# Half of the Strassen differences of a fused attention + MoE kernel taken by GpSimd instead of VectorE

## Chip, cores and metric

One core of a Trainium2 chip. The metric is the device time of one execution in microseconds, from the first to the last instruction on the core with what lies around them; lower is better.

## What is computed

Three layers follow each other. The first is a linear attention: softmax over the head's own 64 columns of q, softmax of k over the sequence, then `q (k^T v)`.

```python
q_s = exp(q - max(q)); q_s = q_s / (sum(q_s) + 1e-9)          # over the head dimension
k_s = exp(k - max(k)); k_s = k_s / (sum(k_s) + 1e-9)          # over the sequence
x   = einsum(q_s, einsum(k_s, v))      # 8 x 8 heads, 576 positions, 64 columns -> 4608 x 512
h   = x @ moe_w_in;   y = (max(h, 0) ** 2) @ moe_w_out        # 512 -> 2048 -> 512
h   = y @ moe2_w_in;  out = elu(h) @ moe2_w_out               # 512 -> 2048 -> 512
```

All of it is float32. A product in float32 is made of three fast products: each operand is split into a high part (rounded by ScalarE) and a low part (what is left, by VectorE), and hi·hi, hi·lo and lo·hi are added up in PSUM.

## The kernel before, in words

The 4608 tokens are cut into nine blocks of 512 (t = 0 to 8). Block 0 goes alone; blocks 1 and 2, 3 and 4, 5 and 6, 7 and 8 are pairs. The first layer's up-projection (`up`, lines 539 to 558) makes G = relu(h)² of a block: 16 tiles of 128 rows by 512 tokens. In a pair these are four quarters, B11 and B21 of the left block (rows 0 to 1023 and 1024 to 2047), B12 and B22 of the right one, each in four pieces of 128 × 1024 (k = 0 to 3).

The down-projection of a pair is done by Strassen-Winograd's scheme with seven products in place of eight. Its right-hand operands are B11, B21, B22 and four differences, taken by `t_sum(to, k)` (line 617), piece by piece:

- T3 = B22 − B12, into a buffer of its own
- T1 = B12 − B11, into B12's place
- T2 = B22 − T1, into B11's place (B11 has been multiplied by then)
- T4 = B21 − T2, into B21's place (B21 has been multiplied by then)

The seven products are 56 **units** (u = 0 to 55), eight of each, in the order T3, T1, B11, B22, T2, B21, T4 (`SEVEN`, line 606). One unit (`unit`, line 1156) does this: `u_mm` (line 652), six matmuls of 512 columns on TensorE (PE) with the weights that `u_load` fetched; the differences that `pair_steps` (line 706) put on this unit; then `u_split(t, u + 2)` (line 642), which makes the operands of the unit after next: `uh` on ScalarE (ACT), then `ul` = x − uh on VectorE (DVE). `uh` and `ul` have three buffers each, so `uh` of unit u can be written once unit u − 3 is through PE.

The order of the work on each engine is written out by hand: the program order is the queue of each engine. Between the units stand steps of the attention of later blocks (`extras`: q and k and v loads, `q_max`, `q_sub`, `q_norm` on DVE, transposes and small products on PE) and, in the last pair, the first steps of the second layer (`x2_sum`, `x2_split`). GpSimd (POOL) has memsets (`v_load`, line 245, and `kv_mm`, line 279) and the issue of some DMAs. `v_load` is issued in two halves: two memsets on POOL, then the load on the queue of SP.

The numbers that the change touches stand in `pair_steps`: the units on which each piece of T1, T2 and T4 is put. T2's piece k is read by `u_split` of units 32 + 2k and 33 + 2k, T4's by that of units 48 + 2k and 49 + 2k. A piece of T2 overwrites what `u_split` of units 16 + 2k and 17 + 2k read, a piece of T4 what that of 40 + 2k and 41 + 2k read.

Of the kernel before, what the change touches and what calls it, by code (L numbers as in the profile page):

```python
# [13 lines left out]
ALU = mybir.AluOpType  # L14
# [6 lines left out]
def tile_attention_moe_moe2(  # L21
# [18 lines left out]
    nc = tc.nc  # L40
# [42 lines left out]
    def xf_slot(i, name):  # L83

        return keep.tile([P, 2 * TB], F32, tag=f"xf{i}", name=name)
# [336 lines left out]
    def attention(t):  # L422

        slots, put = plan()
        new = [b for b, _, _ in pieces(t) if b not in begun]
        begun.update(new)

        far = t > 1
        for b in new:
            for p in range(NP):  # L430
                for i, f in (
                    (0, kt_load), (2, k_max), (5, k_load), (5, v_load), (8, k_row), (8, k_sub), (9 + far, k_exp),
                    (11 + far, kv_mm), (11 + far, kv_sum), (11 + far, kv_inv), (11 + 2 * far, kv_out),
                ):
                    put(i + 4 * p, f, b, p)
        for s in range(NS):
            put(s // 2, q_load, t, s)
            for i, f in (
                (2, q_max), (3, q_sub), (4 + far, q_exp), (5 + 2 * far, q_sum), (6 + 2 * far, q_eps),
                (7 + 2 * far, q_inv), (7 + 2 * far, q_norm),  # L440
            ):
                put(i + 5 * s, f, t, s)
        turns = ((26, 28), (27, 29), (28, 30), (29, 31)) if far else ((23, 25), (25, 27), (27, 29), (28, 29))
        for p, (i, j) in enumerate(turns):
            put(j, x_mm, t, p)
            put(i, x_tr, t, p)
        return slots
# [169 lines left out]
    def t_sum(to, k):  # L617
        if to == "T3":
            x = xf_slot(k % 2, f"T3_{k}").rearrange("p (i n) -> p i n", n=TB)
            a, b = bq["B22", k], bq["B12", k]  # L620
        elif to == "T1":
            x = a = bq["B12", k]
            b = bq["B11", k]
        elif to == "T2":
            x, a, b = bq["B11", k], bq["B22", k], bq["T1", k]
        else:
            x = a = bq["B21", k]
            b = bq["T2", k]
        nc.vector.tensor_tensor(x, a, b, op=ALU.subtract)
        bq[to, k] = x  # L630

    UNITS = {4: "T3", 3: "T1", 0: "B11", 6: "B22", 2: "T2", 1: "B21", 5: "T4"}
# [73 lines left out]
    def pair_steps(t, last):  # L706

        steps = {}

        def put(u, f, *a):  # L710
            steps.setdefault(u, []).append((f, a))

        for to, us in (("T3", (None, None, None, 2)), ("T1", (3, 5, 7, 9)), ("T2", (17, 19, 21, 23)), ("T4", (44, 46, 48, 50))):
            for k, u in enumerate(us):
                if u is not None:
                    put(u, t_sum, to, k)
        put(9, u_keep, t, 4, 0, None)
        put(20, u_v, t)
        put(25, u_keep, t, 0, 0, 1)
        put(33, u_keep, t, 6, 1, 2)  # L720
        if not last:
            put(40, u_keep, t, 2, 0, 3)
        for m in range(2):
            if last:
                put(40 + m, u_out, t, 6, 0, 0, t + 1, m)
                put(42 + m, u_out, t, "v", 0, 1, t + 1, m)
                put(51 + m, u_out, t, 0, 1, 0, t, m)
        if last:
            put(27, u_move, t)
        else:  # L730
            for p, u in enumerate((51, 53, 55, 55)):
                put(u, x_split, 0, t + 2, p)
        return steps
# [333 lines left out]
    with tc.manual_schedule():  # L1067
# [21 lines left out]
        x = attention(PAIRED + 1)  # L1089
        place_all(x[:2], [(0, "c", NSL - 2)])  # L1090
        place_all(x[2:], firsts[PAIRED][:-2])
        for t in range(PAIRED, NB - 2, 2):
            seconds = [(t, "s", s) for s in range(NU // 2)]
            x = attention(t + 2)
# [3 lines left out]
            x = attention(t + 3)  # L1098
# [71 lines left out]
        for t in range(NB):  # L1170
            paired, final = t >= PAIRED, t == NB - 1
            right = paired and (t - PAIRED) % 2 == 1
            for j in range(NFC):
# [4 lines left out]
                if paired:  # L1178
                    if pend:
                        down(*pend.pop(0))  # L1180
                    if right and j in (10, 12):
                        t_sum("T3", (j - 10) // 2)
                    if right and j > 12:

                        u_split(t - 1, j - 13)
                    if right and j == NFC - 1:
                        for u in range(4, 12):
                            u_load(t - 1, u)
                        t_sum("T3", 2)
                    run(extras.get((t, "u", j), ()))  # L1190
                    if right and j == NFC - 3:

                        u_load(t - 1, 2)
                        u_load(t - 1, 3)
                    continue
# [14 lines left out]
            if right:  # L1210
                steps = pair_steps(t - 1, final)
                for u in range(NU - 2 if final else NU):
                    unit(t - 1, u)
# [48 lines left out]
```

## Time and profile before

| | before |
|---|---|
| runs | 1619.37, 1619.68, 1620.75 us |
| median | 1619.68 us |
| profiled execution: span from its first to its last instruction | 1615.5 us |
| what lies around the span, by the median | 4.2 us |
| PE busy | 98% of the span |
| DVE, ACT, POOL busy | 65%, 60%, 6% |
| PE clock granted | full (2.4 GHz) throughout |

The profiled execution gives only its span; its own time is taken as that span and 4.2 us. The four pairs' units lie at about 235 to 320, 421 to 505, 608 to 692 and 784 to 866 us. The second layer follows to the end.

How to read it: a row of the timeline has an instruction's start, its length, its engine, line and operation, what it writes and reads, and in brackets the idle time of the engine before it and what ended that. PEld is the weight load that precedes each matmul; it waits for the operand that the matmul will stream.

### The profile page before, as it was taken

Reading aid. Unit: us, or ns where it says so; the run is one execution under the profiler, and the core shown is the slowest. Engines: PE = TensorE matmul, PEld = TensorE weight load, DVE = VectorE, ACT = ScalarE, POOL = GpSimd, SP = SyncE. Lnnn points to the kernel's source line nnn. Section 1 sums busy time; section 2 is a strip of 40 time slices with the busy share of each in tenths; the row PEclk is TensorE's granted clock in tenths of the full one; section 3 lists DMA queues with packets and bytes.
Section 4 is the critical chain, followed back from the end, with each engine's and each line's share of the span. In section 5 each row is a group of like instructions: output and inputs, shape, how many; then the busy total and the mean of one; then the engine's idle time right before and its main releaser. Section 6 shows DMA issues by size and latency. Waiting matters only on the chain.

```text
span 1615.5 us, 22809 instructions
## 1 busy us (share of the span) xinstructions
PE 1586.3 (98%) x7958; PEld 1350.8 (84%) x7958; DVE 1051.3 (65%) x1658; ACT 974.7 (60%) x1665; POOL 90.6 (6%) x222
## 2 busy tenths in 40 slices
PE   6999999999999999999999999999999999999999
PEld 4778778878788787887888998998989999898997
DVE  7987596777877686773677554555545555555544
ACT  7996655566555675556556655555555565555544
POOL 0001220012101220011000000000000000000000
PEclk9999999999999999999999999999999999999999
DMA  7747566667775685653587555435534543543531
GB/s 264 258 156 246 197 216 198 204 210 237 257 226 174 219 289 164 201 196 111 181 288 259 197 194 173 150 110 154 171 106 143 172 129 117 190 125 109 172 112 59
DMA packets 163953, 296.17 MB, mean 183 GB/s; under 512 B 16384, under 2 KB 52224, under 8 KB 163840
## 3 DMA queue, kind: packets, MB, share of 16 engines
q1 hardware_dynamic: 154240, 263.25, 51.4%
q0 software_dynamic: 9600, 31.46, 4.9%
q8 instruction: 64, 1.05, 0.3%
q14 instruction: 49, 0.40, 0.1%
HBM read 238.03 MB, written 56.62 MB: 182 GB/s over the span
## 4 chain that ended last, share of the span: by engine, by line
PE 82%; DVE 8%; issue 5%; ACT 2%; DMA 2%; POOL 1%; SPq 1%; POOLq 0%; DVEq 0%; ACTq 0%
PE p L816 22%; PE p L661 18%; PE y L878 8%; PE y L879 8%; PE y L877 8%; PE ph L544 5%; PE ph L546 5%; PE ph L545 5%; PE px L400 2%; DVE ks L272 1%; PE pt L379 1%; PE pk L286 1%; DVE mt_wi L111 1%; DVE mt_wi L116 1%; POOL w1s L199 1%
## 5 line engine op out<-in xcount | busy, mean ns | idle before, releaser
L816 PE MATMUL p<-x2h,w 128*128 128x384 f32 x1344 | 359.6, 337 | 0.0
L661 PE MATMUL p<-uh,w 128*128 128x512 f32 x896 | 282.5, 392 | 2.9 <-DMA w<-w1s 2.9
L816 PEld LDWEIGHTS p<-x2h,w 128*128 128x128 f32 x1344 | 245.0, 188 | 4.4 <-ACT h L916 0.2
L544 PE MATMUL ph<-xh,wi0h 128*128 128x512 f32 x576 | 230.7, 401 | 0.1
L879 PE MATMUL y<-wo,g2l 128*128 128x512 f32 x576 | 226.0, 392 | 0.0
L878 PE MATMUL y<-wo,g2h 128*128 128x512 f32 x576 | 225.7, 392 | 0.0
L816 PE MATMUL p<-x2l,w 128*128 128x384 f32 x672 | 225.6, 336 | 0.0
L546 PE MATMUL ph<-xh,wi0l 128*128 128x512 f32 x576 | 225.0, 391 | 0.2 <-DVE wi0l L143 0.2
L545 PE MATMUL ph<-xl,wi0h 128*128 128x512 f32 x576 | 224.4, 390 | 0.0
L877 PE MATMUL y<-wo,g2h 128*128 128x512 f32 x576 | 224.0, 389 | 0.0
L661 PEld LDWEIGHTS p<-uh,w 128*128 128x128 f32 x896 | 168.2, 188 | 38.5 <-ACT uh L648 1.9
L918 DVE TENSOR_TENSOR h<-p,p 128x384 f32<-128x384 f32 x144 | 79.6, 553 | 183.1 <-PE p L816 181.9
L648 ACT ACTIVATE uh<-B 128x512 fp32r<-128x512 f32 x192 | 121.2, 632 | 109.4 <-PE p L661 63.7
L908 ACT ACTIVATE p<-p 128x384 f32<-128x384 f32 x144 | 69.9, 486 | 187.2 <-PE p L816 187.2
L649 DVE TENSOR_TENSOR ul<-B,uh 128x512 fp32r<-128x512 f32 x192 | 131.2, 690 | 69.3 <-ACT uh L648 68.3
L661 PE MATMUL p<-ul,w 128*128 128x512 f32 x448 | 175.3, 391 | 0.2
L553 ACT ACTIVATE B<-ph 128x512 f32<-128x512 f32 x128 | 76.2, 595 | 117.0 <-PE ph L546 116.4
L816 PEld LDWEIGHTS p<-x2l,w 128*128 128x128 f32 x672 | 126.2, 188 | 3.9
L544 PEld LDWEIGHTS ph<-xh,wi0h 128*128 128x128 f32 x576 | 109.2, 189 | 23.1 <-issue 0.9
L546 PEld LDWEIGHTS ph<-xh,wi0l 128*128 128x128 f32 x576 | 108.1, 188 | 24.1 <-DVE wi0l L143 1.1
L545 PEld LDWEIGHTS ph<-xl,wi0h 128*128 128x128 f32 x576 | 108.3, 188 | 22.8 <-issue 0.7
L879 PEld LDWEIGHTS y<-wo,g2l 128*128 128x128 f32 x576 | 108.1, 188 | 22.8
(127 smaller groups left out, 2372.1 us busy)
## 6 DMA issues: line engine op xcount, KB each, us to landing
w<-w2s SPq DMA_DIRECT2D x336, 256.0 KB, 3.0
w<-w1s SPq DMA_DIRECT2D x224, 256.0 KB, 3.4
raw_wi<-wi_dram SPq DMA_DIRECT2D x32, 512.0 KB, 4.2
raw_wo<-wo_dram SPq DMA_DIRECT2D x32, 512.0 KB, 4.0
ks<-k_dram SPq DMA_DIRECT2D x32, 320.0 KB, 4.7
vr<-v_dram SPq DMA_DIRECT2D x32, 320.0 KB, 5.6
kt<-kt_dram SPq DMA_DIRECT2D x32, 288.0 KB, 3.8
q<-q_dram SPq DMA_DIRECT2D x36, 256.0 KB, 4.7
```

The costliest lines, as they stand in the source:

```text
L544: nc.tensor.matmul(ph, hi[:, c], xh[p], start=(p == 0), stop=False)
L545: nc.tensor.matmul(ph, hi[:, c], xl[p], start=False, stop=False)
L546: nc.tensor.matmul(ph, lo[:, c], xh[p], start=False, stop=(p == NP - 1))
L553: nc.scalar.activation(g, ph, AF.Relu)
L648: nc.scalar.activation(hi, x, AF.Copy)
L649: nc.vector.tensor_tensor(lo, x, f32(hi), op=ALU.subtract)
L661: nc.tensor.matmul(accs[side, m], w[:, s, m], x, start=(new and (j, s) == (0, 0) and x is hi), stop=(j == NG - 1 and s == 1), skip_group_c ...
L816: nc.tensor.matmul(acc, w[:, s, k], x[:, k], start=(begin and (k, s) == (0, 0) and x is hi), stop=((k, s) == (1, 1)), skip_group_check=not ...
L877: nc.tensor.matmul(y2[c], gh[:, cs], hi, start=first, stop=False)
L878: nc.tensor.matmul(y2[c], gh[:, cs], lo, start=False, stop=False)
L879: nc.tensor.matmul(y2[c], gl[:, cs], hi, start=False, stop=last)
L918: nc.vector.tensor_tensor(h, part[add], part["bank", i], op=ALU.add)
```

## The change

T2 and T4 (eight pieces in each pair, 32 in all) are subtracted by GpSimd. T1 and T3 stay on VectorE. T4's pieces are put on units 40, 42, 44 and 46 in place of 44, 46, 48 and 50.

```diff
-        nc.vector.tensor_tensor(x, a, b, op=ALU.subtract)
+        eng = nc.gpsimd if to in ("T2", "T4") else nc.vector
+        eng.tensor_tensor(x, a, b, op=ALU.subtract)
         bq[to, k] = x
...
-        for to, us in (("T3", (None, None, None, 2)), ("T1", (3, 5, 7, 9)), ("T2", (17, 19, 21, 23)), ("T4", (44, 46, 48, 50))):
+        for to, us in (("T3", (None, None, None, 2)), ("T1", (3, 5, 7, 9)), ("T2", (17, 19, 21, 23)), ("T4", (40, 42, 44, 46))):
```

The queues of PE, ACT and SP keep their order. DVE, the first pair, units 40 to 52 before (`B_1_` are B21's pieces, `ul_41` the low part for unit 41, `q` and `qz` attention):

```order
L649 TENSOR_TENSOR ul_41_3226<-B_1_0_1818,uh_41_3225 128x512
L362 RECIPROCAL qz_0_3169<-qz_0_3169 128x8
L366 TENSOR_TENSOR q_0_2995<-q_0_2995,qz_0_3169 128x512
L649 TENSOR_TENSOR ul_42_3248<-B_1_1_1891,uh_42_3247 128x512
L649 TENSOR_TENSOR ul_43_3263<-B_1_1_1891,uh_43_3262 128x512
L649 TENSOR_TENSOR ul_44_3275<-B_1_2_1968,uh_44_3274 128x512
L649 TENSOR_TENSOR ul_45_3287<-B_1_2_1968,uh_45_3286 128x512
L629 TENSOR_TENSOR B_1_0_1818<-B_1_0_1818,B_1_0_1486 128x1024
L649 TENSOR_TENSOR ul_46_3300<-B_1_3_2044,uh_46_3299 128x512
L649 TENSOR_TENSOR ul_47_3312<-B_1_3_2044,uh_47_3311 128x512
L629 TENSOR_TENSOR B_1_1_1891<-B_1_1_1891,B_1_1_1582 128x1024
L649 TENSOR_TENSOR ul_48_3325<-B_1_0_1818,uh_48_3324 128x512
```

The same place on DVE in the changed kernel:

```order
L650 TENSOR_TENSOR ul_41_3226<-B_1_0_1818,uh_41_3225 128x512
L362 RECIPROCAL qz_0_3169<-qz_0_3169 128x8
L366 TENSOR_TENSOR q_0_2995<-q_0_2995,qz_0_3169 128x512
L650 TENSOR_TENSOR ul_42_3249<-B_1_1_1891,uh_42_3248 128x512
L650 TENSOR_TENSOR ul_43_3264<-B_1_1_1891,uh_43_3263 128x512
L650 TENSOR_TENSOR ul_44_3277<-B_1_2_1968,uh_44_3276 128x512
L650 TENSOR_TENSOR ul_45_3289<-B_1_2_1968,uh_45_3288 128x512
L650 TENSOR_TENSOR ul_46_3302<-B_1_3_2044,uh_46_3301 128x512
L650 TENSOR_TENSOR ul_47_3314<-B_1_3_2044,uh_47_3313 128x512
L650 TENSOR_TENSOR ul_48_3327<-B_1_0_1818,uh_48_3326 128x512
```

The 1024-column subtractions are gone from between the low parts. They stand on POOL, here in the first pair (`B_1_0_1486` and its like are T2 in B11's place, `B_1_0_1818` and its like T4 in B21's; `vr` and `kvs` are attention tiles):

```order
 L295 MEMSET kvs_3_2784 128x128
+L630 TENSOR_TENSOR B_1_0_1486<-B_2_0_2362,B_2_0_2112 128x1024
+L630 TENSOR_TENSOR B_1_1_1582<-B_2_1_2438,B_2_1_2163 128x1024
+L630 TENSOR_TENSOR B_1_2_1649<-B_2_2_2500,B_2_2_2218 128x1024
+L630 TENSOR_TENSOR B_1_3_1736<-B_2_3_2582,B_2_3_2283 128x1024
 L249 MEMSET vr_0_3111 128x5
 L250 MEMSET vr_0_3111 128x5
 L249 MEMSET vr_1_3231 128x5
 L250 MEMSET vr_1_3231 128x5
+L630 TENSOR_TENSOR B_1_0_1818<-B_1_0_1818,B_1_0_1486 128x1024
+L630 TENSOR_TENSOR B_1_1_1891<-B_1_1_1891,B_1_1_1582 128x1024
+L630 TENSOR_TENSOR B_1_2_1968<-B_1_2_1968,B_1_2_1649 128x1024
```

Eight subtractions have come into POOL's queue, four of them ahead of memsets for the next v loads, with no DMA issue between them.

## Rows read from the trace of the kernel before

**Rows 1.** The page: busy time by engine, and the chain that ended last, by engine.

```profile
PE 1586.3 (98%) x7958; PEld 1350.8 (84%) x7958; DVE 1051.3 (65%) x1658; ACT 974.7 (60%) x1665; POOL 90.6 (6%) x222
...
PE 82%; DVE 8%; issue 5%; ACT 2%; DMA 2%; POOL 1%; SPq 1%; POOLq 0%; DVEq 0%; ACTq 0%
```

**Rows 2.** Waits of PE's weight loads, 230 to 866 us: total, times, longest.

```profile
PEld p L661 <- DVE ul L649: 3.7, 12, 0.5
```

**Rows 3.** Waits of PE's weight loads in the fourth pair, 806 to 866 us.

```profile
PEld p L661 <- DVE ul L649: 1.0, 3, 0.5
```

**Rows 4.** Timeline of PEld: first weight load for the low part of units 42 and 44.

```profile
673.09 0.19 PEld L661 LDWEIGHTS p<-ul,w 128*128 128x128 f32 x1
...
675.81 0.19 PEld L661 LDWEIGHTS p<-ul,w 128*128 128x128 f32 x1
```

**Rows 5.** Timeline of DVE, third pair: low parts of units 41 to 45 (L649).

```profile
669.87 0.69 DVE L649 TENSOR_TENSOR ul<-B,uh 128x512 fp32r<-128x512 f32 x1 [0.67 <-ACT uh L648]
670.48 0.20 DVE L362 RECIPROCAL qz<-qz 128x8 f32<-128x8 f32 x1
670.71 0.69 DVE L366 TENSOR_TENSOR q<-q,qz 128x512 f32<-128x512 f32 x1
671.32 0.68 DVE L649 TENSOR_TENSOR ul<-B,uh 128x512 fp32r<-128x512 f32 x1
672.73 0.69 DVE L649 TENSOR_TENSOR ul<-B,uh 128x512 fp32r<-128x512 f32 x1 [0.72 <-ACT uh L648]
673.95 0.69 DVE L649 TENSOR_TENSOR ul<-B,uh 128x512 fp32r<-128x512 f32 x1 [0.54 <-ACT uh L648]
675.31 0.69 DVE L649 TENSOR_TENSOR ul<-B,uh 128x512 fp32r<-128x512 f32 x1 [0.67 <-ACT uh L648]
```

**Rows 6.** Timeline of ACT: high parts of units 44, 45 and 47.

```profile
673.29 0.63 ACT L648 ACTIVATE uh<-B 128x512 fp32r<-128x512 f32 x1 [0.59 <-PE p L661]
674.65 0.63 ACT L648 ACTIVATE uh<-B 128x512 fp32r<-128x512 f32 x1 [0.73 <-DVE ul L649]
...
677.37 0.63 ACT L648 ACTIVATE uh<-B 128x512 fp32r<-128x512 f32 x1 [0.73 <-PE p L661]
```

**Rows 7.** Groups of DVE by line and shape: count, busy us, mean ns, idle before.

```profile
L649 DVE TENSOR_TENSOR ul<-B,uh 128x512 fp32r<-128x512 f32 x192 | 131.2, 690 | 69.3 <-ACT uh L648 68.3
...
L629 DVE TENSOR_TENSOR B<-B,B 128x1024 f32<-128x1024 f32 x48 | 58.5, 1219 | 0.0
...
L353 DVE TENSOR_REDUCE qz<-q 128x8 f32<-128x512 f32 x34 | 23.0, 676 | 0.0
```

**Rows 8.** Groups of POOL by line and shape, the same columns.

```profile
L295 POOL MEMSET kvs<- 128x128 f32 x32 | 6.7, 217 | 9.5 <-PE px L400 9.5
L249 POOL MEMSET vr<- 128x5 f32 x32 | 3.7, 118 | 175.7 <-PE pk L286 127.1 <-issue 48.6
...
masks.py:199 POOL TENSOR_SCALAR_AFFINE_SELECT ident<-ident 128x128 f32<-128x128 f32 x1 | 0.3, 288 | 0.1
```

**Rows 9.** Timeline of DVE, first pair: T2's third piece, low parts of units 23, 24.

```profile
272.94 1.22 DVE L629 TENSOR_TENSOR B<-B,B 128x1024 f32<-128x1024 f32 x1
274.08 1.29 DVE L649 TENSOR_TENSOR ul<-B,uh 128x512 fp32r<-128x512 f32 x2
```

**Rows 10.** Timeline of all engines, first pair: weight load for the low part of unit 24.

```profile
276.08 0.19 PEld L661 LDWEIGHTS p<-ul,w 128*128 128x128 f32 x1
```

**Rows 11.** Timeline of DVE, fourth pair: low parts of units 17 and 18.

```profile
807.22 0.69 DVE L649 TENSOR_TENSOR ul<-B,uh 128x512 fp32r<-128x512 f32 x1 [0.67 <-ACT uh L648]
808.58 0.69 DVE L649 TENSOR_TENSOR ul<-B,uh 128x512 fp32r<-128x512 f32 x1 [0.67 <-ACT uh L648]
```

**Rows 12.** Timeline of POOL, first pair: memset for the v load that follows.

```profile
234.29 0.13 POOL L249 MEMSET vr<- 128x5 f32 x1
```

**Rows 13.** Timeline of SP, first pair: that v load is issued.

```profile
288.07 0.56 SPq L251 DMA_DIRECT2D vr<-v_dram x1
```

## The prediction

> **What bounds the kernel.** I read the page first: PE is busy for 98% of the span and makes 82% of the chain that ended last; DVE has 8% of that chain although it is busy for 65% [rows 1]. So work taken off DVE is worth only what PE waits for it. The view of waits says how much that is: over all four pairs the weight loads of the units waited for a low part 12 times, 3.7 us together [rows 2], and the largest share of it, 1.0 us, lies in the fourth pair [rows 3].
>
> Then the timelines, for the spare time. In the third pair a weight load for a low part comes at 673.09 for unit 42 and 675.81 for unit 44 [rows 4]: a unit takes PE 1.36 us. The low part of unit 44 starts at 673.95, ends at 674.64 [rows 5], and is wanted at 675.81 [rows 4]: 1.17 us to spare. That is the margin of nearly every low part; DVE works one unit ahead and cannot get further, since the high part in front of it waits for PE to free a buffer (673.29, released by PE) [rows 6]. A low part that comes over 1.17 us late stops PE.
>
> I take anything over 0.2% (3.2 us) as measurable for this kernel.
>
> **What the change removes.** 32 subtractions of 1.22 us leave DVE (39 us of its busy time) [rows 7]. They delay the next low part by under the margin in most places, so PE gains only the waits that they caused. I put that at 1.0 us, the fourth pair's sum [rows 3], of at most 3.7 us [rows 2]; the other waits lie mostly at T1 and at attention steps, which stay.
>
> **What it adds: the price on GpSimd.** No row shows a subtraction there, so it is bounded. A memset of 128 columns takes 217 ns and one of 5 columns 118 ns [rows 8]: 99 ns for 123 columns, 0.80 ns per column for one stream. The one operation that reads and writes, 128 columns, takes 288 ns [rows 8]: 170 ns over the small memset, 1.33 ns per column. From below it cannot be better than DVE's 1.22 us [rows 7] by anything seen here. Two reads with the write hidden are 0.12 + 1024 × 1.6 ns = 1.74 us; three streams one after the other are 0.12 + 1024 × 2.4 ns = 2.56 us; twice the read-and-write rate is 2.85 us. I take the middle of the two stream counts, **2.15 us**, which is also near 0.12 + 1024 × (1.33 + 0.80) ns = 2.30 us.
>
> **What it adds: the company of DVE.** The other unknown is what DVE's low parts do while GpSimd subtracts. From below: nothing, they keep their 0.69 us. From above: one of the two waits until the other is through. A fact of the rows speaks for the upper end: DVE takes two SBUF operands of 512 columns in 690 ns and reduces a single one in 676 ns [rows 7], so it reads two streams at once, and any path that GpSimd's two reads share with the second of them is taken. GpSimd's instructions beside the low parts so far are memsets, which read nothing [rows 8], so no row refutes it. I take the upper end. The Trainium skill says the same of this very pairing ("SBUF — State Buffer", section "Who interferes with whom"): a VectorE instruction with two SBUF inputs contends with a GpSimd instruction that reads SBUF, and the one that issues second is blocked until the first is done; no row of this trace shows it.
>
> The place matters, because GpSimd's start is tied to DVE's. A piece of T4 overwrites what the low part of unit 41 + 2k read, so it starts when that ends, just when DVE turns to the next one. Replayed on the third pair, with 2.15 us:
>
> - The low part of unit 41 ends at 670.56 [rows 5]. GpSimd holds from 670.60 to 672.75. `q_norm` (670.71) and the low part of unit 42 (671.32) [rows 5] are both two-input operations; they run after it, and the latter ends at 674.05 in place of 672.00. Its weight load is due at 673.09 [rows 4]: PE loses 1.0 us.
> - The low parts of 43 and 44 (high part ready at 673.92 [rows 6], as its buffer was freed by unit 41) follow without a gap, to 675.27. The second piece runs then, to 677.42. The high part of 45 has moved by the 1.0 us that PE lost, from 674.65 [rows 6] to 675.65; its low part ends at 678.11 and is due at 675.81 + 1.36 + 1.0 = 678.17: no loss.
> - The low part of 46 follows, the third piece goes from 678.72 to 680.87, the low part of 47 (high part 677.37 [rows 6] plus 1.0) ends at 681.56, due at 675.81 + 3 × 1.36 + 1.0 = 680.89: 0.7 us lost.
> - The fourth piece likewise, before the low part of 49: 0.7 us lost.
>
> That is 2.4 us for four pieces of T4. The other pairs have the same order of work there (in the fourth an `x2_split` stands in the place of `q_norm`): 4 × 2.4 = 9.6 us.
>
> T2: in the first three pairs PE does attention's transposes and products between these units, so the first three pieces have room. The fourth has not: with T2's third piece off DVE, the low part of unit 23 runs at 272.94 in place of 274.08 [rows 9], GpSimd goes from 273.65 to 275.80, the low part of unit 24 ends at 276.5, wanted at 276.08 [rows 10]: 0.4 us, three times 1.2 us. In the fourth pair there is no such room: the low part of unit 17 ends at 807.91, that of 18 is due to start at 808.58 [rows 11] and ends at 810.8 in place of 809.27, 1.5 us late for a margin of 1.17: 0.3 us, and then 0.7 us for two of the three that follow, as above: 1.7 us.
>
> **What is queued behind.** GpSimd's queue is in order. The memset of the next v tile, at 234.29 [rows 12], now stands behind four pieces of T2, whose last ends at about 276. Its load is issued by SP at 288.07 [rows 13], so 12 us are left. No DMA issue stands among the pieces. In the replay T4's fourth piece ends at 684.3, as unit 49 begins; it is read for unit 54, whose operands are made during unit 52. Four units later it would not have fitted.
>
> **The sum.** 9.6 + 1.2 + 1.7 − 1.0 = **+11.5 us**. On the profiled execution: 1615.5 + 11.5 = 1627.0 us of span; with the 4.2 us around it, which make up the median of the runs, 1631.2 us. With 1.74 us in place of 2.15 the first loss is 0.6 us and the later ones nearly vanish: about +3 us, 1623. With 2.56 us a piece and the two low parts behind it (1.3 us) take 3.9 us where two units have 2.72: 1.1 us lost per piece, 4.4 for a batch, five batches 22 us, 1.3 us more from T2, less 1.0: +22 us, 1642. At N = 2048 the Trainium skill gives 4497 ns for such an addition ("GPSIMD Engine Reference", section "Performance versus the Vector engine"); an estimate of half of it, 2.25 us, would put the sum at about +14 us.
>
> **The rivals.**
>
> *A. They share without loss (not slower).* DVE's low parts keep their rate beside GpSimd, or lose less than the 1.17 us that each has to spare; GpSimd takes the longer time itself, and with six units (8.2 us) between a T4 piece and its reader nobody waits. Then only the removed waits are seen: 1619.7 − 1.0, 1619 us, no change. For it: the margin, and that each piece has half a stage of time. Against it: DVE's two streams at full rate. It decides if the added delay of one low part stays under 1.17 us.
>
> *B. GpSimd is far slower.* At 2.85 us and more, T4's last piece comes after unit 52 and PE waits for it as well: 1.5 us per piece, 20 pieces, and some 2 us per pair for the last: 1655 us or more.
>
> *C. DVE was the real limit (faster).* If all 3.7 us [rows 2] and knock-on waits went, 1616 us. Against it: only part of those waits stand at T2 and T4.
>
> **How the numbers follow.** Forecast 0.48 (1623 to 1642); A 0.44; B 0.05; C 0.03. The forecast and A stand nearly level, since no row shows the two engines reading together; the forecast is ahead by DVE's two streams. Slower by over 0.2%: 0.48 + 0.05 = 0.53; within: 0.44; faster: 0.03. The range reaches from A's time, 1618.5 us, to 1642 us and leaves out B and C. The forecast's own range is 1623 to 1642.
>
> **What would show it.** Right: 32 subtractions on POOL at L630, their starts 3.6 to 4 us apart at T4; DVE's low parts beside them either starting only at GpSimd's end or stretched to over 2 us; and PE's weight loads waiting for `ul` at units 42, 47 and 49 of each pair, 10 to 15 us more in all. A is right if the low parts keep 0.69 us and those waits stay under 4 us. B shows as waits for `uh` on POOL at units 52 to 55. The forecast is wrong if GpSimd's subtraction takes under 1.6 us or if low parts run inside it.

## The result

The changed kernel took 1635.61 us (median of 4 runs, 1635.04 to 1636.42), the kernel before 1619.53 us beside it: a ratio of 1.0098, 95% interval 1.0086 to 1.0111. That is 16.1 us slower (13.9 to 18.0). The forecast was 1631 us with a range of 1618.5 to 1642.

The page of the changed kernel, answering to [rows 1]: span, busy time by engine, and the chain that ended last.

```profile
span 1634.1 us, 22844 instructions
...
PE 1594.5 (98%) x7958; PEld 1351.5 (83%) x7958; DVE 1054.6 (65%) x1626; ACT 974.5 (60%) x1665; POOL 173.2 (11%) x254
...
PE 77%; DVE 11%; issue 5%; ACT 3%; DMA 2%; POOL 1%; SPq 0%; POOLq 0%; ACTq 0%; DVEq 0%
```

DVE has 32 instructions fewer and is yet busy 3 us longer; its share of the chain rose from 8% to 11%. The groups by line and shape say why, POOL first and then DVE (columns as in [rows 7]):

```profile
L630 POOL TENSOR_TENSOR B<-B,B 128x1024 f32<-128x1024 f32 x32 | 83.1, 2597 | 231.4 <-DVE ul L650 162.8 <-DVE qz L362 67.9 <-POOL B L630 0.7
...
L650 DVE TENSOR_TENSOR ul<-B,uh 128x512 fp32r<-128x512 f32 x192 | 168.5, 896 | 80.3 <-ACT uh L649 79.2
```

A low part takes 896 ns in the mean where it took 690 [rows 7]: 37 us more in sum, which eats up nearly all of the 39 us that the 32 subtractions had taken on DVE. The low parts that stand clear of GpSimd are still 0.69 us long; the others are up to 2.9 us. Here is the place of the replay, the first piece of T4 in the third pair (timeline of DVE, answering to [rows 5], then of POOL, then of PE's weight loads, answering to [rows 4]):

```profile
680.04 0.69 DVE L650 TENSOR_TENSOR ul<-B,uh 128x512 fp32r<-128x512 f32 x1 [0.67 <-ACT uh L649]
680.65 0.20 DVE L362 RECIPROCAL qz<-qz 128x8 f32<-128x8 f32 x1
680.88 0.69 DVE L366 TENSOR_TENSOR q<-q,qz 128x512 f32<-128x512 f32 x1
681.48 2.90 DVE L650 TENSOR_TENSOR ul<-B,uh 128x512 fp32r<-128x512 f32 x1
```

```profile
680.87 2.96 POOL L630 TENSOR_TENSOR B<-B,B 128x1024 f32<-128x1024 f32 x1 [22.61 <-DVE qz L362]
685.12 2.73 POOL L630 TENSOR_TENSOR B<-B,B 128x1024 f32<-128x1024 f32 x1 [1.29 <-DVE ul L650]
688.54 2.72 POOL L630 TENSOR_TENSOR B<-B,B 128x1024 f32<-128x1024 f32 x1 [0.69 <-DVE ul L650]
691.96 2.72 POOL L630 TENSOR_TENSOR B<-B,B 128x1024 f32<-128x1024 f32 x1 [0.70 <-DVE ul L650]
```

```profile
684.43 0.19 PEld L662 LDWEIGHTS p<-ul,w 128*128 128x128 f32 x1 [1.22 <-DVE ul L650]
...
691.87 0.19 PEld L662 LDWEIGHTS p<-ul,w 128*128 128x128 f32 x1 [0.75 <-DVE ul L650]
...
695.28 0.19 PEld L662 LDWEIGHTS p<-ul,w 128*128 128x128 f32 x1 [0.78 <-DVE ul L650]
```

`q_norm` came first, the other way round than in the replay, and ended at 681.57. GpSimd's row begins at 680.87 but lasts 2.96 us, 0.57 us more than the 2.39 us of a piece that meets nobody: it waited. The low part of unit 42 was next in DVE's queue and its row of 2.90 us ends at 684.38, 0.55 us after GpSimd's end at 683.83: it waited through the whole subtraction and then did its work. A row's length here includes the wait, on both engines. The three weight loads that PE had to wait for are those of units 42, 47 and 49, the three that the replay named.

Over the four pairs (waits of PE's weight loads, 230 to 886 us, answering to [rows 2], then the whole fourth pair, 797.9 to 883.3 us):

```profile
PEld p L662 <- DVE ul L650: 19.7, 25, 1.7
```

```profile
PEld p L662 <- DVE ul L650: 7.8, 8, 1.7
```

3.7 us have become 19.7: 16.0 us more, close to the difference between the medians. Of the 7.8 us, 0.9 lie at the pair's first units, as they do before; from about unit 16 on, where [rows 3] begins, 1.0 us has become 6.9. Counted by the length of the units' own matmuls, from the first one's start to the last one's in each unit, the four pairs are 2.9, 3.2, 2.8 and 5.6 us longer, 14.5 in all.

The two spans differ by 18.6 us, 4 more than the units. Most of that has nothing to do with the change. Up to the first unit, where the two programs are alike, the profiled execution of the changed kernel is 3.5 us longer than that of the kernel before: PE's granted clock stood at 1.2 GHz for 6.8 us in block 0. A profile of the same queues with the full clock there (T4 on its old units, below) is 0.3 us longer up to that point. The stretch, after:

```profile
101.10:107.90 6.80, 5.68 (x14) 4.54 (x15) 6.29 (x13) 4.91 (x11) 0.00 (x0) 0.50 0.52 178
```

(The columns are the stretch, its length, busy us and instructions of PE, PEld, DVE, ACT and POOL, the granted clock, DMA share and GB/s.) PE did 14 matmuls there, and 29 in the same stretch of the kernel before, whose clock was full. What lies around a span is 1.7 us in this execution (1635.84 us for a span of 1634.1), not the 4.2 us taken for the kernel before; if it is as much there, the execution that was profiled before was some 2.5 us faster than the median. The forecast was added to the median and is not touched by this.

### The profile page after: what moved, and what is told of

It is laid out like the page before. It is cut to its first block, busy times and chain, and to the rows that moved or that the text cites. A ratio compares the mean times of both kernels' runs of the same rounds, so it can differ in the third digit from the quotient of the medians.

```text
span 1634.1 us, 22844 instructions
## 1 busy us (share of the span) xinstructions
PE 1594.5 (98%) x7958; PEld 1351.5 (83%) x7958; DVE 1054.6 (65%) x1626; ACT 974.5 (60%) x1665; POOL 173.2 (11%) x254
## 4 chain that ended last, share of the span: by engine, by line
PE 77%; DVE 11%; issue 5%; ACT 3%; DMA 2%; POOL 1%; SPq 0%; POOLq 0%; ACTq 0%; DVEq 0%
PE p L817 22%; PE p L662 13%; PE y L879 8%; PE y L880 8%; PE y L878 8%; PE ph L544 5%; PE ph L546 5%; PE ph L545 5%; DVE ul L650 4%; PE px L400 2%; PE pt L379 1%; DVE ks L272 1%; ACT uh L649 1%; PE pk L286 1%; DVE mt_wi L111 1%
## 5 line engine op out<-in xcount | busy, mean ns | idle before, releaser
L650 DVE TENSOR_TENSOR ul<-B,uh 128x512 fp32r<-128x512 f32 x192 | 168.5, 896 | 80.3 <-ACT uh L649 79.2
L649 ACT ACTIVATE uh<-B 128x512 fp32r<-128x512 f32 x192 | 121.2, 632 | 123.7 <-PE p L662 96.4
```

The source lines that it names most:

```text
L649: nc.scalar.activation(hi, x, AF.Copy)
L650: nc.vector.tensor_tensor(lo, x, f32(hi), op=ALU.subtract)
```

## The experiments

The theory: a VectorE operation with two SBUF inputs and a GpSimd operation that reads SBUF exclude each other for the whole of the one that came first. The rivals: GpSimd's work costs by its sum, whatever it does; the earlier place of T4 is what costs; every piece costs alike. Every experiment's time is told beside the kernel before on the same chip, as a ratio with its 95% interval; waits are those of PE's weight loads for `ul`, 230 to 886 us.

### GpSimd busy as long, but only writing

```diff
-        eng = nc.gpsimd if to in ("T2", "T4") else nc.vector
-        eng.tensor_tensor(x, a, b, op=ALU.subtract)
+        if to in ("T2", "T4"):
+            for _ in range(3):
+                nc.gpsimd.memset(x, 0.01)
+        else:
+            nc.vector.tensor_tensor(x, a, b, op=ALU.subtract)
```

> In place of each of the 32 subtractions GpSimd writes the same 128x1024 tile three times (memset), so it is busy as long but reads nothing; T2 and T4 are left out of the computation. Theory (a two-input VectorE operation and a GpSimd operation that reads exclude each other): low parts keep 0.69 us beside the memsets, the waits of weight loads for ul stay under 4 us in all, time 1617 to 1621 us. Rival (any GpSimd instruction at that place costs it, by its length or by the semaphore hand-over): 1630 us or more, with low parts of 2 us and longer.

Measured: 1619.09 us, ratio 0.999 (0.9977 to 1.0003). Waits: 2.6 us. The same place (timeline of DVE, then of POOL):

```profile
670.65 0.69 DVE L366 TENSOR_TENSOR q<-q,qz 128x512 f32<-128x512 f32 x1
671.26 0.68 DVE L653 TENSOR_TENSOR ul<-B,uh 128x512 fp32r<-128x512 f32 x1
672.66 0.69 DVE L653 TENSOR_TENSOR ul<-B,uh 128x512 fp32r<-128x512 f32 x1 [0.72 <-ACT uh L652]
673.89 0.69 DVE L653 TENSOR_TENSOR ul<-B,uh 128x512 fp32r<-128x512 f32 x1 [0.54 <-ACT uh L652]
```

```profile
670.56 3.89 POOL L631 MEMSET B<- 128x1024 f32 x4 [21.55 <-DVE ul L653]
```

GpSimd works without a break from 670.56 on and every low part beside it keeps its length. It also bounds what the removal of the 32 subtractions from DVE was worth: nothing that the interval tells from zero. The price of the change is not GpSimd's time or the hand-over by semaphores.

### GpSimd reading one stream

```diff
-        eng = nc.gpsimd if to in ("T2", "T4") else nc.vector
-        eng.tensor_tensor(x, a, b, op=ALU.subtract)
+        if to in ("T2", "T4"):
+            nc.gpsimd.tensor_copy(x, b)
+        else:
+            nc.vector.tensor_tensor(x, a, b, op=ALU.subtract)
```

> In place of each subtraction GpSimd copies its second operand (one SBUF read and one write of 1024 columns); the subtractions of T2 and T4 are left out of the computation. Theory (reading is what excludes): two-input operations of VectorE beside a copy still end only after it; a copy takes 0.9 to 1.5 us, so a low part is late by at most 0.9 us of the 1.17 that it has to spare, the longest one in the third pair's T4 is 1.2 to 2.0 us, and the time is 1618 to 1622 us. Rival (only a GpSimd operation with two reads collides): low parts keep 0.69 us beside the copies, same time; the rows, not the time, tell the two apart.

Measured: 1620.10 us, ratio 0.9994 (0.9983 to 1.0006). Waits: 3.0 us. DVE, then POOL:

```profile
673.78 1.57 DVE L366 TENSOR_TENSOR q<-q,qz 128x512 f32<-128x512 f32 x1
...
677.02 1.24 DVE L652 TENSOR_TENSOR ul<-B,uh 128x512 fp32r<-128x512 f32 x1 [0.47 <-ACT uh L651]
```

```profile
673.77 1.04 POOL L630 COPY B<-B 128x1024 f32<-128x1024 f32 x1 [23.57 <-DVE qz L362]
676.68 1.04 POOL L630 COPY B<-B 128x1024 f32<-128x1024 f32 x1 [1.87 <-DVE ul L652]
```

`q_norm` started 0.01 us behind the copy and ended at 675.35, 0.54 us after the copy's end; the low part that started at 677.02 ended at 678.26, 0.54 us after the second copy's. So one read stream on GpSimd is enough to hold a two-input operation of DVE. It cost no time: a hold of 1.04 us is less than the 1.17 us that a low part mostly has to spare, and the low part of unit 42 here, behind `q_norm`, still ended 0.21 us ahead of its weight load.

The other side of the pair shows in the changed kernel itself. In its fourth pair `u_v` (L691), whose second input lies in PSUM, falls into a hold (DVE, then POOL):

```profile
828.12 1.27 DVE L691 TENSOR_TENSOR v<-k,p 128x512 f32<-128x512 f32 x2
829.31 1.71 DVE L650 TENSOR_TENSOR ul<-B,uh 128x512 fp32r<-128x512 f32 x1
```

```profile
827.73 2.74 POOL L630 TENSOR_TENSOR B<-B,B 128x1024 f32<-128x1024 f32 x1 [0.69 <-DVE ul L650]
```

The two additions with one SBUF input run at their usual length inside GpSimd's subtraction; the low part behind them, with two, ends only after GpSimd, at 831.02. In these rows the chip thus does what the Trainium skill states ("SBUF — State Buffer", section "Who interferes with whom"), in all three points: two inputs contend with reads, not with writes, and one input does not contend.

### The engine alone, the place alone

The diff of the first is the change without its second part (T4 on units 44, 46, 48 and 50, on GpSimd), that of the second is the second part alone (40, 42, 44 and 46, on VectorE).

> The engine alone is changed: T2 and T4 on GpSimd, T4 put back on units 44, 46, 48 and 50. Theory: nothing else stands in GpSimd's queue there, so a piece starts when the low part that it overwrites has been made, wherever it was put; the queues are the same as in the changed kernel, and the time is 1633 to 1638 us with the first T4 piece of the third pair again at about 681 us. Rival (my prediction's remark that T4 would not fit four units later): the pieces start some 5.4 us later, PE waits for uh at units 52 to 55, and the time is 1640 us or more.

Measured: 1634.24 us, ratio 1.0096 (1.0079 to 1.0112). Waits: 19.4 us. POOL in the third pair:

```profile
677.41 2.96 POOL L630 TENSOR_TENSOR B<-B,B 128x1024 f32<-128x1024 f32 x1 [22.62 <-DVE qz L362]
681.66 2.72 POOL L630 TENSOR_TENSOR B<-B,B 128x1024 f32<-128x1024 f32 x1 [1.29 <-DVE ul L650]
685.08 2.73 POOL L630 TENSOR_TENSOR B<-B,B 128x1024 f32<-128x1024 f32 x1 [0.69 <-DVE ul L650]
```

The lengths and the gaps are those of the changed kernel to 0.01 us; all of it is 3.5 us earlier, as the slow stretch in block 0 is absent. The second half of the change does nothing on GpSimd: that engine is idle there, so a piece starts when the last reader of its place is through, wherever it was written. The instructions of each queue stand in the same order in the two programs.

> The place alone is changed: all differences on VectorE, T4 on units 40, 42, 44 and 46. Theory: each 1.22 us subtraction delays one low part by less than the 1.17 us that it has to spare, except beside q_norm at unit 42 (0.69 + 1.22 us, under 0.3 us lost in a pair): 1618 to 1622 us. Rival (the earlier place is what costs): 1630 us or more.

Measured: 1621.45 us, ratio 1.0012 (1.0000 to 1.0024). Waits: 6.1 us. On VectorE the place does count, a little: the units are 2.1 us longer than before, 1.6 of them in the fourth pair at units 42 to 46, where DVE has other work. It is not what cost 16 us.

### By part and by pair

> T2 alone is on GpSimd; T4 is on VectorE and on its old units. Theory: by the units' own lengths in the changed kernel T2 cost 0.52, 0.54, 0.40 and 1.49 us in the four pairs, so 2 to 4 us: 1621 to 1624 us. Rival (each of the 32 pieces costs the same): half of the 16 us, 1627 to 1628 us.

(T2 on GpSimd; T4 as before.) Measured: 1621.91 us, ratio 1.0009 (0.9999 to 1.0020), units 3.0 us longer, waits 6.9 us. T2 is the cheaper half by far: 3 of 14.5 us by the units.

> On GpSimd only the first three pieces of T2 in the first three pairs (9 of the 32), where PE has attention's products between the units. Theory: a low part has over 2 us to spare there, so a hold of 2.4 us costs nothing, and VectorE's 11 us less are worth nothing either: 1618 to 1621 us, waits for ul 3.2 to 4 us. Rival (each piece costs what the mean of the 32 did, 0.5 us): 1624 us.

```diff
-        nc.vector.tensor_tensor(x, a, b, op=ALU.subtract)
+        eng = nc.gpsimd if to == "T2" and k < 3 and not st.get("last") else nc.vector
+        eng.tensor_tensor(x, a, b, op=ALU.subtract)
...
```

Measured: 1619.60 us, ratio 0.9994 (0.9983 to 1.0006). Waits: 3.4 us. These nine pieces take 2.38 us each and cost nothing. PE does attention's work between these units, so the low parts lie far apart: in each pair two of the three pieces meet no low part at all, and the third meets one at its end and delays it by 0.25 us, which leaves it 1.7 us to spare. So a place with room is free; a full hold against two microseconds to spare was not tried. They gain nothing either.

> The change, in the first three pairs alone; the fourth as before. Theory: the units' own lengths say 2.9, 3.2 and 2.8 us for these pairs, so +9 us and 1628 to 1631 us, with waits for ul at units 24, 42, 47 and 49 and nowhere else new. Rival (the pieces cost alike in all pairs): three quarters of 16 us, 1631 to 1633 us.

(The whole pieces of the change, T4 at its new place, in the first three pairs.) Measured: 1627.47 us, ratio 1.0046 (1.0029 to 1.0062), 7.5 us. Waits: 13.3 us; the units of the three pairs are 2.9, 3.1 and 2.8 us longer, those of the fourth pair as before. The forecast of 1628 us and up was high by half a microsecond; the pairs' own sums held. The fourth pair alone costs 5.6 us, twice another's.

### The length of a hold, and the pace of holds

```diff
+        if to in ("T2", "T4"):
+            for j in range(2):
+                nc.gpsimd.tensor_tensor(x[:, j], a[:, j], b[:, j], op=ALU.subtract)
...
```

> Each piece is subtracted on GpSimd in two halves of 512 columns, one after the other: the same columns, half the hold. Theory (the length of one hold against the margin, and the pace of holds against VectorE's work): a half takes 1.2 to 1.3 us and delays a low part by 0.6 us, under the margin, but two halves and two low parts still want some 3.9 us of every 2.72, so about half of the loss stays: 1624 to 1631 us. Rival (the GpSimd time in sum is what costs): 1634 to 1638 us, as the changed kernel. Other rival (the hold alone counts): 1621 us or less.

Measured: 1629.12 us, ratio 1.0049 (1.0031 to 1.0068). Waits: 16.2 us, 30 times, the longest 1.0 us. T4 of the third pair (two rows of POOL, then one of DVE that holds two low parts):

```profile
682.13 1.74 POOL L631 TENSOR_TENSOR B<-B,B 128x512 f32<-128x512 f32 x1
...
683.83 1.74 POOL L631 TENSOR_TENSOR B<-B,B 128x512 f32<-128x512 f32 x1
```

```profile
682.64 3.48 DVE L653 TENSOR_TENSOR ul<-B,uh 128x512 fp32r<-128x512 f32 x2
```

With the shorter hold, half of the loss stays by the time (0.49% of 0.98%) and two thirds by the units' lengths (10.0 of 14.5 us). The pace says why: a half that meets nobody takes 1.29 us, and here halves and low parts take turns, one of each in 1.70 us (682.13 to 683.83) where PE wants a low part every 1.36 us. Of the 1.74 us of such a row, 0.45 us are GpSimd's own wait.

```diff
+        if to in ("T2", "T4"):
+            for j in range(2):
+                for _ in range(3):
+                    nc.gpsimd.memset(idle, 0.0)
+                nc.gpsimd.tensor_tensor(x[:, j], a[:, j], b[:, j], op=ALU.subtract)
...
```

> As the halves, with three memsets of a scratch tile of 256 columns before each half, which only write: they space the halves by some 1 us more. Theory: with holds under the margin and a pace that leaves VectorE its two low parts, nothing is lost: waits for ul under 4 us in all, 1617 to 1622 us, no faster than the kernel before by over 0.2%. Rival (the GpSimd time in sum, now larger): 1634 us or more.

Measured: 1625.60 us, ratio 1.0037 (1.0024 to 1.0049). Waits: 10.3 us. (`idle` is a scratch tile of 256 columns.) A miss: above the forecast, though the units are 5.9 us longer in all where the halves without memsets made them 10.0 us longer. By pair they are 0.1, 0.6, 0.6 and 4.6 us longer. So the spacing works in three pairs, and the fourth keeps its loss. There (DVE, then POOL):

```profile
852.06 0.67 DVE L703 TENSOR_TENSOR k<-k,p 128x512 f32<-128x512 f32 x1
852.66 1.72 DVE L656 TENSOR_TENSOR ul<-B,uh 128x512 fp32r<-128x512 f32 x1
854.30 0.67 DVE L703 TENSOR_TENSOR k<-k,p 128x512 f32<-128x512 f32 x1
854.90 1.72 DVE L656 TENSOR_TENSOR ul<-B,uh 128x512 fp32r<-128x512 f32 x1
```

```profile
852.54 1.29 POOL L634 TENSOR_TENSOR B<-B,B 128x512 f32<-128x512 f32 x1
853.77 1.04 POOL L633 MEMSET idle<- 128x256 f32 x3
854.78 1.30 POOL L634 TENSOR_TENSOR B<-B,B 128x512 f32<-128x512 f32 x1
```

DVE has an output addition (L703) between two low parts. While DVE does that one, which needs no second stream, GpSimd begins its half (852.54, 854.78), and the next low part meets it nearly from its start and is held: 2.24 us from low part to low part, 0.88 over what PE wants. The replay in the prediction had taken T4 of the fourth pair to run like that of the third.

> The spaced halves in the first three pairs alone; in the fourth T2 and T4 are back on VectorE and on their old units. Theory: what the spaced halves still lost stood in the fourth pair, whose T4 stretch has four further VectorE operations of 0.68 us and an x2_split, so that no pace of holds leaves VectorE room; without it 1618 to 1623 us, waits for ul under 6 us. Rival (a spaced half costs the same in every pair): three quarters of the 0.37%, 1624 to 1625 us.

Measured: 1620.38 us, ratio 0.9999 (0.9987 to 1.0011). Waits: 4.8 us. The fourth pair is as in the kernel before. The spaced halves in the first three pairs alone are level with the kernel before, with 24 of the 32 subtractions on GpSimd. The 7.5 us of the whole pieces in the same three pairs are gone, by a shorter hold and a wider pace and no other edit.

## Why the prediction was right

The direction and the mechanism were right, and the sum came out at 11.5 us for a measured 16.1 (13.9 to 18.0). By its own steps:

- **What bounds.** PE, with DVE's work worth only the waits it causes: right. With GpSimd only writing, DVE's 39 us less were worth nothing that the interval shows. The 1.17 us to spare is the median in the kernel before, not the margin of nearly every low part: of 224, 75 have under 1.0 us and 39 over 1.3. At T4 it told cheap holds from dear ones: a hold of 1.04 us cost nothing, one of 2.39 us did.
- **The price on GpSimd.** 2.15 us was taken, 2.39 us is what a piece takes that meets nobody; the second estimate, 2.30 us, was nearer. (The two bounds around 2.15 come to 1.76 and 2.58 us as they are written, not 1.74 and 2.56.) A half takes 1.29 us, so it is 0.19 us and 2.15 ns per column, 2.7 times memset's 0.80 ns [rows 8].
- **The company of DVE.** The upper end was taken, that one waits out the other. Right, and shown from both sides. The trace of before gave it little support, so 0.44 for rival A was fair; the copy shows that even a single read stream on GpSimd holds DVE.
- **T4, first three pairs.** 2.4 us a pair were replayed, at units 42, 47 and 49. In the first three pairs the units' excess at T4 is 2.40, 2.38 and 2.39 us, at those units. That is closer than the terms deserve, and partly luck: the price was 0.24 us too low, but a piece and the low part behind it follow each other in 2.26 + 0.55 = 2.81 us (681.57 to 683.83 to 684.38 above), less than the 3.08 us of their two lengths alone, where the replay had added 2.15 + 0.69 = 2.84. The starts of the pieces lay 4.25, 3.42 and 3.42 us apart, where 3.6 to 4 us had been named as the sign.
- **T2, first three pairs.** 0.4 us each at unit 24, measured 0.57, 0.56 and 0.40 at that unit. Right.
- **The fourth pair.** Here lies the term that was mis-sized: 2.4 us for its T4, measured 4.2 us; the 1.7 us for its T2 were 1.5. The replay carried the third pair's order over ("the other pairs have the same order of work there"). The losses there are 1.2, 1.6 and 1.5 us, at units 42, 44 and 46, not at 42, 47 and 49. The fourth pair has four output additions (L697) between the low parts of units 42 to 46, and at units 44 and 46 GpSimd begins beside such an addition and need not wait, so that the next low part is held for nearly the whole piece (changed kernel, DVE, then POOL):

```profile
859.98 0.67 DVE L697 TENSOR_TENSOR k<-k,p 128x512 f32<-128x512 f32 x1
860.58 2.56 DVE L650 TENSOR_TENSOR ul<-B,uh 128x512 fp32r<-128x512 f32 x1
```

```profile
860.20 2.39 POOL L630 TENSOR_TENSOR B<-B,B 128x1024 f32<-128x1024 f32 x1 [1.89 <-DVE ul L650]
```

- **What is removed.** 1.0 us was credited. With GpSimd only writing, the waits fell from 3.7 to 2.6 us and the units became 0.3 us shorter: right in size by the one count, high by 0.7 us by the other.
- **What is queued behind.** The v loads were not late: the first memset behind T2 came at 279.62, its load was issued at 292.17. Nor did PE wait longer for high parts (2.0 us, before 1.9), which would have been the sign of rival B. But the sentence that T4 would not have fitted four units later is wrong: with T4 on its old units GpSimd starts at the same moment. The place in the program orders an idle engine's queue and does not time it.

Where the 1.6 us between the units' 14.5 and the medians' 16.1 lie stays open; the interval of the medians holds both. The clock may have a share (last section): the four runs of the changed kernel all had a mean granted clock of 0.998 of full speed, and that of the runs beside them is not on record.

## What to carry to other kernels

Before work goes from VectorE to GpSimd, ask of both sides what they read: subtractions with two SBUF inputs run one after the other on the two engines, at 2.39 us on GpSimd for 1.22 on VectorE, while writes on GpSimd, and operations of VectorE whose second input lies in PSUM, ran beside the other engine at their usual length. The price of a hold is set by the spare time of the next small operation in VectorE's queue, not by the busy shares (65% and 6% looked like room). If such work has to move, make a piece so short that the delay it causes stays under that spare time (a half piece delayed a low part by up to 1.1 us, a whole one by 2.2), and space the pieces so that VectorE gets all its turns between them; on an idle queue, a later place in the program does not space them. Ask first what the move can win: here nothing, even where it cost nothing.

## What had not been expected of the hardware

PE's granted clock falls to 1.2 GHz for 3.4 or 6.8 us in some executions and not in others of the same order of work. Eight of the twelve profiles show it, each at one or both of two places: beginning at 99 to 102 us (block 0, the stretch shown above) or at 537 to 541 us. The second place gives its price: in the four profiles with 3.4 us of it there, the way from the second pair's last unit to the third pair's first is 1.5 to 1.6 us longer than in the kernel before, and in the others it is the same to 0.1 us. What PE did before it fell was nearly the same in both programs (76.6 us busy of the 81 us before it in the changed kernel, 76.4 in the kernel before, where it did not fall); why one execution is caught and another isn't stays open. Single runs of the kernel before, 1617.7 to 1624.2 us on one chip, go with it: the twelve with a mean granted clock of 0.999 of full speed took 1619.4 us in the mean, the seven with 0.997 took 1623.2. That is as large as the smaller effects of this study, which is why those were read from waits and unit lengths as well as from times.
